# Where late attention stands on TensorE between feed-forward products, and how far ahead h products may run

## The chip, the core and the metric

The kernel runs on one core of a Trainium2 chip. A core has five engines that each go through their own instructions in order and wait for each other by semaphores: TensorE (PE) multiplies matrices into PSUM banks, VectorE (DVE), ScalarE (ACT) and GpSimd (POOL) work on tiles, and SyncE (SP) issues the transfers here. The metric is the device time of the whole program in microseconds (us); lower is better.

## What is computed

Attention with a learned decay over 4 x 8 heads of 576 x 64, and two feed-forward products behind it on 2304 tokens:

```python
def _attn_ref(q, k, v, f):
    scores = scale * np.matmul(q, k.transpose(0, 1, 3, 2))
    cum = np.cumsum(np.log(np.clip(f, 0.0001, 1.0)), axis=-1)
    decay = cum[:, :, :, None] - cum[:, :, None, :]
    scores = np.where(causal, -1000000000.0, scores + decay)
    scores = scores - np.max(scores, axis=-1, keepdims=True)
    attn = np.exp(scores)
    attn = attn / (np.sum(attn, axis=-1, keepdims=True) + 1e-09)
    return np.matmul(attn, v)

x = attn_out.transpose(0, 2, 1, 3).reshape(B * S, H * D)
h = np.maximum(x @ w_in, 0.0);  x = h * h @ w_out          
h = x @ w_in2;  g = h - np.tanh(h);  out = g @ w_out2
```

## The kernel before

**Stages.** The first feed-forward runs in eight blocks of 288 tokens (numbers 0 to 7; two blocks to a batch of eight heads), the second in five blocks of up to 512 tokens behind them. A block has 16 steps, one for each 128 of the 2048 inner columns. A step has twelve h products (L139, into the tile hp) and, two steps later, twelve y products (L165, into four tiles yp). Twelve, since every float32 factor is split into a rounded high part and a rest: high x high, low x high, high x low, over four blocks of the contraction. ACT makes relu and square of hp into gh and tmp (L149 to L151), and gl = tmp - gh (L101, the helper for every rest) is made on POOL in blocks 0 and 1 and on DVE from block 2 on. Four of a step's twelve y products read gl. hp has a single bank of PSUM in blocks 0 to 5 and three after that; gh and gl have three buffers.

**Attention beside it.** Block 2 needs the heads of batch 1, block 4 those of batch 2, block 6 those of batch 3; so attention of the later heads runs beside the feed-forward of the earlier batches. It is written as a Python generator that yields after each *piece*. A late head k (17 to 31) takes five pieces: scores of query tile 4; scores of tile 3 and the turn of tile 4; split_p(0) of head k-1, scores of tile 2, turn 3; split_p(1) of head k-1, scores of tiles 1 and 0, turn 2; turns 1 and 0, put(k), pv(k-1). After the fifth get(k) is issued. The score products are L443 and L444 into s_ps.

**From head to head.** The softmaxed P of a late head is turned in 32 x 32 blocks on DVE into T (L473, L476, L470), put stores T to DRAM (p_d, 1 MB, L479), get loads it back turned in four transfers into PTl (L485), split_p rounds it on POOL into PTh (L90) and takes the rest on DVE into PTl (L101), and pv multiplies both with V on PE into o_ps (L516 to L521). PTl, PTh and T each have one buffer, so a head's load waits for the P x V of the one before. s_ps, o_ps and o0_ps share three banks. ACT and DVE take the result out (xt L88, xs L531), and after every second head the pair's x is split and stored (x_d, L409 and L410); block 2's first load of x (xhl, L706) is issued on SP among the gets.

**What sets the order.** advance() calls as many pieces as a pace (cuts, ENDS) asks for, twice in each step of blocks 0 to 5: once behind the h products, once behind the y products. A1 is the number of the first late piece (116), total 196. The program is built twice. What is emitted before block 2 (MARK) keeps the order of the first building; behind that a planner with a timeline orders each engine's instructions, within data dependences and within the bounds that tc.issue_after sets: an instruction inside it stands behind the given one on the engine's queue. PEI[n] holds the last PE instruction emitted by the end of piece n, and SLK[j] is the slack of block j: its h products stand behind PEI[pieces so far - 1 - SLK[j]]; None sets no bound. Before the change nothing else bounds where the attention's own PE instructions stand:

```python
 660          while cnt[0] < min(to, total):
 661              next(ga, None)
 662              PEI[cnt[0]] = next(x for x in reversed(nc.cur_bb.bb.instructions) if x.engine == EngineType.PE)
 663              cnt[0] += 1
```

## Time and profile before

| | |
|---|---|
| median of 3 runs | 1089.9 us (1088.54 to 1091.76) |
| the profiled execution's own time | 1093.25 us |
| its span in the trace | 1091.5 us |
| PE busy | 1032.9 us, 95% of the span |
| DVE, ACT, POOL busy | 641.9, 526.2, 250.8 us |
| PTl loads in the chain that ended last | 6% of the span |

The span is the profiled execution from the first to the last instruction, 1.75 us shorter than its time. The trace says what each engine did when, and what the time in which it did nothing was waiting for. In the windows PEclk is the clock granted to PE as a share of 2.4 GHz; a mean between 0.5 and 1 is a mixture of the two levels, 1.2 and 2.4 GHz. Waits are named by the engine and line that waited, and by what it waited for; the chain of waits goes back from the end of the program to what released each step.

### The profile page before, as it was taken

How to read it: one execution, taken by the hardware profiler on the slowest of the kernel's cores; microseconds unless marked ns; L12 is line 12 of the kernel's file. 1: busy time of each engine (PE TensorE's matmuls, PEld its weight loads, DVE VectorE, ACT ScalarE, POOL GpSimd, SP SyncE). 2: the span in 40 equal slices, each digit the busy share in tenths (PEclk: the TensorE clock that was granted, in tenths of full speed). 3: DMA queues.
4: the chain of work that ended last, by engine and by line, in shares of the span. 5: the costliest groups of instructions: out<-in, count | busy, mean ns of one | idle time of the engine just before them, and what ended most of it. 6: DMA issues, size and time to landing. Idle time of an engine off the chain costs nothing.

```text
span 1091.5 us, 16915 instructions
## 1 busy us (share of the span) xinstructions
PE 1032.9 (95%) x6048; PEld 900.9 (83%) x6048; DVE 641.9 (59%) x1663; ACT 526.2 (48%) x1221; POOL 250.8 (23%) x357
## 2 busy tenths in 40 slices
PE   3989999999998899999989999999999999999998
PEld 3576678888998788888989999888888888888898
DVE  7799987777877677877624747763222222222232
ACT  5787777765564545646425657432222222222222
POOL 4244455555545343433310000000000000000000
PEclk9899999999999899999989999999999999999999
DMA  6556643223955657846448069100300300110010
GB/s 203 219 149 183 175 149 135 88 80 132 319 176 168 197 146 244 247 136 208 160 119 303 1 233 331 64 0 1 116 1 1 116 1 1 39 39 1 1 39 21
DMA packets 63301, 134.83 MB, mean 124 GB/s; under 512 B 6416, under 2 KB 31568, under 8 KB 61168
## 3 DMA queue, kind: packets, MB, share of 16 engines
q1 hardware_dynamic: 63216, 133.74, 38.8%
q8 instruction: 48, 0.79, 0.3%
q14 instruction: 37, 0.30, 0.1%
HBM read 93.94 MB, written 39.78 MB: 123 GB/s over the span
## 4 chain that ended last, share of the span: by engine, by line
PE 57%; DMA 9%; DVE 4%; POOL 1%; SPq 1%; ACT 1%; issue 1%; POOLq 0%; ACTq 0%; DVEq 0%
PE yp L165 27%; PE hp L139 27%; DMA PTl<-p_d 6%; DMA p_d<-T 3%; DVE PTl L101 2%; PE o_ps L519 2%; SPq L485 1%; POOL PTh L90 1%; DVE gl L101 1%; DVE T L473 1%; DVE QA L101 0%; PE s_ps L443 0%; PE s_ps L444 0%; ACT P L426 0%; PE o_ps L516 0%
## 5 line engine op out<-in xcount | busy, mean ns | idle before, releaser
L139 PE MATMUL hp<-xhl,w 128*128 128x288 f32 (+2 forms) x2496 | 453.3, 329 | 2.4 <-ACT tmp L149 1.2
L139 PEld LDWEIGHTS hp<-xhl,w 128*128 128x128 f32 x2496 | 387.6, 191 | 39.1 <-ACT tmp L149 1.7
L165 PE MATMUL yp<-ghl,w 128*128 128x512 f32 (+1 forms) x960 | 216.2, 374 | 0.0
L165 PE MATMUL yp<-gh,w 128*128 128x288 f32 x1024 | 200.6, 301 | 0.0
L165 PEld LDWEIGHTS yp<-ghl,w 128*128 128x128 f32 x960 | 168.4, 188 | 34.5
L154 DVE TENSOR_TENSOR tmp<-hp,tmp 128x512 f32<-128x512 f32 (+1 forms) x80 | 51.0, 638 | 206.6 <-ACT tmp L153 206.6
L165 PEld LDWEIGHTS yp<-gh,w 128*128 128x128 f32 x1024 | 162.4, 192 | 2.1 <-issue 1.0
L153 ACT ACTIVATE tmp<-hp 128x512 f32<-128x512 f32 (+1 forms) x80 | 44.4, 555 | 225.4 <-PE hp L139 225.4
L165 PE MATMUL yp<-gl,w 128*128 128x288 f32 x512 | 133.9, 300 | 2.6 <-DVE gl L101 1.7
L149 ACT ACTIVATE tmp<-hp 128x288 f32<-128x288 f32 x128 | 51.9, 407 | 116.2 <-PE hp L139 103.1
L426 ACT ACTIVATE P<-P,ST 128x320 f32<-128x320 f32 (+4 forms) x151 | 84.6, 562 | 34.1 <-DVE ST L417 32.9
L165 PEld LDWEIGHTS yp<-gl,w 128*128 128x128 f32 x512 | 90.6, 190 | 5.1 <-DVE gl L101 2.7
L430 POOL TENSOR_SCALAR P<-P,ST 128x448 f32<-128x448 f32 (+4 forms) x88 | 59.8, 681 | 102.8 <-DVE ST L429 61.4
L101 DVE TENSOR_TENSOR ghl<-tmp,ghl 128x512 fp32r<-128x512 f32 (+1 forms) x80 | 51.1, 638 | 47.4 <-ACT ghl L88 47.1
L101 DVE TENSOR_TENSOR gl<-tmp,gh 128x288 fp32r<-128x288 f32 x96 | 47.6, 497 | 48.0 <-ACT tmp L151 47.6
L417 DVE CUSTOM_DVE_ANT_0 P<-s_ps,mk 128x320 f32<-128x320 f32 (+3 forms) x151 | 63.6, 432 | 19.1 <-PE s_ps L444 12.2
L101 DVE TENSOR_TENSOR PTl<-PTl,PTh 128x512 fp32r<-128x512 f32 (+1 forms) x64 | 51.9, 841 | 35.1 <-POOL PTh L90 35.1
L88 ACT ACTIVATE ghl<-tmp 128x512 fp32r<-128x512 f32 (+1 forms) x80 | 47.2, 590 | 49.6 <-DVE tmp L154 49.6
L90 POOL TENSOR_SCALAR PTh<-PTl 128x512 fp32r<-128x512 f32 (+1 forms) x64 | 46.5, 752 | 56.4 <-DMA PTl<-p_d 55.7
L150 ACT ACTIVATE gh<-tmp 128x288 fp32r<-128x288 f32 x128 | 56.6, 443 | 4.0 <-PE yp L165 1.0
L151 ACT ACTIVATE tmp<-tmp 128x288 f32<-128x288 f32 x128 | 56.2, 440 | 2.4
L88 ACT ACTIVATE w<-wst 128x512 fp32r<-128x512 f32 x64 | 40.0, 625 | 29.5 <-DVE wst L123 29.4
(121 smaller groups left out, 1261.5 us busy)
## 6 DMA issues: line engine op xcount, KB each, us to landing
raw<-in_w_dram SPq DMA_DIRECT2D x64, 512.0 KB
p_d<-T SPq DMA_DIRECT2D x16, 1024.0 KB
PTl<-p_d SPq DMA_DIRECT2D x64, 256.0 KB
R<-in_qk_dram SPq DMA_DIRECT2D x24, 576.0 KB
xhl<-y_d SPq DMA_DIRECT2D x16, 512.0 KB
xhl<-x_d SPq DMA_DIRECT2D x14, 576.0 KB
y_d<-yst SPq DMA_DIRECT2D x14, 576.0 KB
VR<-in_v_dram SPq DMA_DIRECT2D x32, 160.0 KB
```

Of the source, the lines that this page charges most:

```text
L88: eng.activation(out, in_, AF.Copy)
L90: eng.tensor_scalar(out, in_, 1.0, 1.0, ALU.mult, ALU.mult)
L101: eng.tensor_tensor(out, in_, hi.bitcast(F32), ALU.subtract)
L139: nc.tensor.matmul(ps, w[:, k * 128:(k + 1) * 128], xk, start=(jj == 0), stop=(jj == 11))
L149: nc.scalar.activation(tmp, ps, AF.Relu)
L150: nc.scalar.activation(gh, tmp, AF.Square)
L151: nc.scalar.activation(tmp, tmp, AF.Square)
L154: nc.vector.tensor_tensor(tmp, ps, tmp, ALU.subtract)
L165: nc.tensor.matmul(yp[m][:, :n], w[:, c], x, start=(i == 0 and j == 0), stop=(i == NF - 1 and j == 2))
L417: nc.vector.tensor_tensor_reduce(p[:rows, a:b], ps[:rows, :b - a], mk[:rows, o:o + b - a], -0.125, 3.0e38 if mn is None else mn, ALU.add, ...
L426: nc.scalar.activation(p[:rows, :n], p[:rows, :n], AF.Exp, bias=mn, scale=-1.0, accum_out=st[:rows, 1, t:t + 1])
L430: by(n_by).tensor_scalar(p[:rows, :n], p[:rows, :n], st[:rows, 3, t:t + 1], 1.0, ALU.mult, ALU.mult)
```

## The change

Two things. SLK becomes 3 for blocks 3, 4 and 5; blocks 3 and 4 had 8, block 5 had no bound. And the late pieces are called inside tc.issue_after of the last PE instruction that stood in the program when advance() was called, which is a product of the feed-forward step just emitted; so their PE instructions stand behind it. last_pe() is the expression that was written out before.

```diff
-SLK = (None, 8, 3, 8, 8, None)
+SLK = (None, 8, 3, 3, 3, 3)
...
+    def last_pe():
+        return next(x for x in reversed(nc.cur_bb.bb.instructions) if x.engine == EngineType.PE)
+
     def advance(to):
+        ff = last_pe()
         while cnt[0] < min(to, total):
-            next(ga, None)
-            PEI[cnt[0]] = next(x for x in reversed(nc.cur_bb.bb.instructions) if x.engine == EngineType.PE)
+            with tc.issue_after(ff) if cnt[0] >= A1 else ExitStack():
+                next(ga, None)
+            PEI[cnt[0]] = last_pe()
             cnt[0] += 1
```

Both kernels have the same instructions; only their order on the engines differs, on PE from the end of block 1 on. In the rows below a name's number tells buffers and steps apart; the shape at the end is that of the moving operand, and xN is a count of like rows.

PE at the start of block 2, before the change. yp_2338 is the last y product of block 1, hp_3377 the first h of block 2, o_ps_3504 the P x V of head 16, s_ps scores of head 17:

```order
L165 MATMUL yp_2338<-gl_3360,w15_1_1949 128x288
L519 MATMUL o_ps_3504<-PTh_1610,VH_3416 128x512
L521 MATMUL o0_ps_3514<-PTl_1611,VR_3088 64x64
L443 MATMUL s_ps_3547<-QA_3409 128x320
L444 MATMUL s_ps_3547<-QB_3243 128x320
L519 MATMUL o_ps_3504<-PTh_1610,VH_3416 128x512
L519 MATMUL o_ps_3504<-PTl_1611,VH_3416 128x512
L139 MATMUL hp_3377<-xhl_3297,w0_0_480 128x288 x8
```

And with the change:

```order
L165 MATMUL yp_2338<-gl_3360,w15_1_1949 128x288
L139 MATMUL hp_3377<-xhl_3297,w0_0_480 128x288 x8
L139 MATMUL hp_3377<-xhl_3298,w0_0_480 128x288 x4
L139 MATMUL hp_3432<-xhl_3297,w1_0_610 128x288 x8
L139 MATMUL hp_3432<-xhl_3298,w1_0_610 128x288 x4
L443 MATMUL s_ps_3460<-QA_3168 128x192
L444 MATMUL s_ps_3460<-QB_3069 128x192
L443 MATMUL s_ps_3468<-QA_3168 128x64
L444 MATMUL s_ps_3468<-QB_3069 128x64
L519 MATMUL o_ps_3504<-PTh_1610,VH_3416 128x512 x2
```

Two steps of block 2's h products, and scores, now stand ahead of head 16's P x V.

PE at the end of block 3, before. gl_5163 belongs to its step 13, o_ps_5308 is the P x V of head 24:

```order
L165 MATMUL yp_4519<-gh_5162,w13_1_1758 128x288 x2
L519 MATMUL o_ps_5308<-PTh_1610,VH_5132 128x512 x2
L521 MATMUL o0_ps_5318<-PTl_1611,VR_4841 64x64
L443 MATMUL s_ps_5375<-QA_5125 128x320
L165 MATMUL yp_4516<-gl_5163,w13_1_1758 128x288
L165 MATMUL yp_4517<-gl_5163,w13_1_1758 128x288
```

And with the change:

```order
L165 MATMUL yp_4516<-gl_5163,w13_1_1758 128x288
L165 MATMUL yp_4517<-gl_5163,w13_1_1758 128x288
L165 MATMUL yp_4518<-gl_5163,w13_1_1758 128x288
L165 MATMUL yp_4519<-gl_5163,w13_1_1758 128x288
L165 MATMUL yp_4516<-gh_5223,w14_1_1855 128x288 x2
...
L165 MATMUL yp_4519<-gl_5224,w14_1_1855 128x288
L519 MATMUL o_ps_5308<-PTh_1610,VH_5132 128x512 x2
```

The y products of steps 13 and 14 now stand ahead of the P x V of head 24, which before stood ahead of step 13's four gl products.

DVE at the same place, before. The four PTl rows are head 24's rests, which need the load of its P and POOL's rounding:

```order
L101 TENSOR_TENSOR PTl_1611<-PTl_1611,PTh_1610 128x4x128
L101 TENSOR_TENSOR gl_5163<-tmp_5161,gh_5162 128x288
L101 TENSOR_TENSOR PTl_1611<-PTl_1611,PTh_1610 128x4x128
L101 TENSOR_TENSOR PTl_1611<-PTl_1611,PTh_1610 128x4x96
L101 TENSOR_TENSOR PTl_1611<-PTl_1611,PTh_1610 128x4x64
L101 TENSOR_TENSOR gl_5224<-tmp_5222,gh_5223 128x288
```

And with the change (T is that of head 25):

```order
L101 TENSOR_TENSOR PTl_1611<-PTl_1611,PTh_1610 128x4x128
L101 TENSOR_TENSOR QA_5465<-R_5168,QA_5465 64x576
L473 STREAM_TRANSPOSE T_1612<-P2_1605 128x3x4x32
L428 TENSOR_SCALAR ST_4922<-ST_4922 128x1
L101 TENSOR_TENSOR PTl_1611<-PTl_1611,PTh_1610 128x4x128
L101 TENSOR_TENSOR PTl_1611<-PTl_1611,PTh_1610 128x4x96
L428 TENSOR_SCALAR ST_4922<-ST_4922 64x1
L101 TENSOR_TENSOR PTl_1611<-PTl_1611,PTh_1610 128x4x64
L101 TENSOR_TENSOR gl_5163<-tmp_5161,gh_5162 128x288
```

gl_5163 has moved from behind the first rest to behind all four.

## Rows read from the trace of the kernel before

**Rows 1.** The page, part 1: busy us of each engine, share, instructions.

```profile
PE 1032.9 (95%) x6048; PEld 900.9 (83%) x6048; DVE 641.9 (59%) x1663; ACT 526.2 (48%) x1221; POOL 250.8 (23%) x357
```

**Rows 2.** Windows of 20 us: stretch, length, busy of PE PEld DVE ACT POOL, PEclk, DMA share, GB/s.

```profile
360.00:380.00 20.00, 15.74 (x92) 14.47 (x91) 13.09 (x37) 7.90 (x22) 9.45 (x11) 0.83 0.66 208
400.00:420.00 20.00, 18.50 (x118) 17.16 (x117) 15.03 (x55) 11.63 (x29) 10.12 (x13) 0.91 0.45 148
440.00:460.00 20.00, 18.02 (x117) 16.97 (x116) 15.89 (x50) 11.00 (x31) 9.12 (x11) 0.91 0.83 271
540.00:560.00 20.00, 16.20 (x90) 14.53 (x89) 7.35 (x15) 4.80 (x11) 4.20 (x6) 0.83 0.37 106
600.00:620.00 20.00, 20.00 (x152) 20.00 (x152) 15.05 (x29) 13.63 (x31) 0.00 (x0) 1.00 0.01 1
```

**Rows 3.** Windows of 5 us, PE alone: stretch, length, busy, PEclk, DMA share, GB/s.

```profile
345.00:350.00 5.00, 4.45 (x27) 1.00 0.00 0
365.00:370.00 5.00, 3.86 (x13) 0.51 0.49 167
```

**Rows 4.** Waits, 262 to 575 us: who waits for whom, us in all, times, longest.

```profile
POOL PTh L90 <- DMA PTl<-p_d: 55.7, 14, 11.7
...
PE o_ps L519 <- POOL PTh L90: 16.6, 9, 4.3
...
PE yp L165 <- DVE gl L101: 1.7, 2, 1.0
```

**Rows 5.** Chain of waits, 320 to 575 us, heads 19 to 21: start, us, what.

```profile
328.85 2.33 POOL PTh L90 x3
...
344.46 0.63 POOL PTh L90
...
352.82 5.11 DMA p_d<-T
...
359.32 5.97 DMA PTl<-p_d
365.47 0.63 POOL PTh L90
```

**Rows 6.** The same chain, head 29.

```profile
517.59 0.63 POOL PTh L90
518.26 0.49 PE o_ps L519
```

**Rows 7.** Timeline of SP's DMA queue, the load of head 29: start, us, what.

```profile
510.04 1.74 SPq L485 DMA_DIRECT2D PTl<-p_d  x4
```

**Rows 8.** Groups by line, 325 to 560 us: busy, mean ns, then idle before.

```profile
L101 DVE TENSOR_TENSOR PTl<-PTl,PTh 128x512 fp32r<-128x512 f32 (+2 forms) x52 | 43.0, 856 | 33.8 <-POOL PTh L90 33.7
...
L101 DVE TENSOR_TENSOR gl<-tmp,gh 128x288 fp32r<-128x288 f32 x48 | 24.8, 517 | 10.8 <-ACT tmp L151 10.6
...
L101 DVE TENSOR_TENSOR QA<-R,QA 64x576 fp32r<-64x576 f32 x10 | 11.6, 1161 | 0.3
```

**Rows 9.** Chain of waits, 540 to 640 us: the last P·V, and block 7.

```profile
561.51 0.43 PE o_ps L519
...
630.59 1.60 PE hp L139 x12
```

**Rows 10.** Timeline of SP's queue: a get, and the loads of x for blocks 2 and 6.

```profile
268.92 1.79 SPq L485 DMA_DIRECT2D PTl<-p_d  x4
...
271.23 0.98 SPq L706 DMA_DIRECT2D xhl<-x_d  x2
...
566.16 1.95 SPq L706 DMA_DIRECT2D xhl<-x_d  x2
```

**Rows 11.** Timeline of PE at the start of block 2: head 16's P·V, block 2's h.

```profile
278.79 0.46 PE L519 MATMUL o_ps<-PTh,VH 128*128 128x512 f32 x1
...
281.12 1.23 PE L139 MATMUL hp<-xhl,w 128*128 128x288 f32 x8
```

## The prediction

> **What bounds the kernel now.** I first read the page's busy shares and its slices. TensorE (PE) is busy 95% of the span, DVE 59%, ACT 48%, POOL 23% [rows 1], so the end is set by PE, and the question is what keeps PE from its products. The slices say where. In blocks 2 to 5, from about 279 to 562 us, late attention and feed-forward share PE; behind 562 us PE is dense (20.00 busy of 20 at 600 us) [rows 2]. In the shared part two things cost time: waits, and stretches in which the granted clock lay below full. 360 to 380 us was busy for 15.74 of 20 us at a mean clock of 0.83 of 2.4 GHz, that is with a part of it at the lower level, 1.2 GHz; the slices at 400 and 440 have 0.91, that at 540 has 0.83 [rows 2]. Those four lose 3.4 + 1.8 + 1.8 + 3.4 = 10.4 us (20 us times what is missing to 1.00). A fall follows a pause: 365 to 370 us, behind the longest wait, has 0.51 [rows 3].
>
> The view of waits names the pauses. Between 262 and 575 us the P·V products (o_ps, L519) wait 16.6 us in nine places for POOL's rounding of P (PTh, L90), the longest 4.3 us, and that rounding itself waits for the load of the turned P back from DRAM (PTl<-p_d, 55.7 us). The second feed-forward products wait 1.7 us for gl on DVE [rows 4]. So the thing that ends last in this part is a loop from head to head: P turned on DVE, stored (put), loaded (get), rounded on POOL, its rest taken on DVE, multiplied on PE.
>
> The chain of waits shows two lengths of that loop. The **long** one runs where the turns and the put of a head stand on DVE behind the rests of the head before. From one rounding to the next it took 15.6 us in one head (328.85 to 344.46) and 21.0 us in the next (to 365.47), of which the put came 8.4 us behind the rounding, its store took 5.1, the load 6.0 [rows 5]. The **short** one runs where the put is long done and only the load waits for the buffer: load issued at 510.04, rounding at 517.59, products at 518.26, some 8 us [rows 6, 7], and with the product ahead of it (2.5 us, eight of 0.49 and less [rows 6]) about 11 from head to head.
>
> PE's own work in this part I count from the order at dense durations: twelve products of 128x288 take 1.60 us [rows 9], a step of h and y 3.2; five blocks of 16 steps from the start of block 2 to that of block 7 make 256 us, the late heads at some 4 us each 58.6, together 314.6. The trace needed 351.8 (278.8, where the P·V of head 16 starts, to 630.6 us [rows 9, 11]). So **37.2 us are lost**, and the order leaves PE's own work as it was. The whole question is what is lost with the new order.
>
> **The change part by part.** Nothing is removed or added; the same instructions stand otherwise on each engine. Before, P·V products and scores slid ahead between feed-forward products as the planner found room; now they stand whole behind the last feed-forward product emitted, and in blocks 3 to 5 h products may no more run ahead than three pieces. Effect one: feed-forward is spread evenly. Own work between the starts of successive P·V was 10.5 to 21 us, uneven; in the new order heads 17 to 31 have 17.8, 17.4, 10.0, 19.0, 13.7, 16.9, 16.9, 18.5, 19.9, 21.6, 20.0, 17.3, 13.6, 17.2, 11.4 (head 22, for one: 2.5 of P·V, 1.6 of scores, four steps of 3.2). That is 11 us more cover in sum, and as much less dense work behind the last head. What each wait becomes is loop minus cover.
>
> *Long loops.* Heads 17, 18, 20, 22, 23 and 30 have the long loop and less cover than it. I take loops of 19.0 to 21.6 us, nearer to the 21.0 than to the 15.6 [rows 5], since in the new order the turns that the put waits for stand behind the rests, with gl among them, in all of these heads: 1.15 + 1.6 + 2.6 + 3.85 + 3.6 + 2.8 = 15.6 us. With 15.6 everywhere nothing is left (0), with 21.0 the sum is 3.2 + 3.6 + 2.0 + 4.1 + 4.1 + 3.8 = 20.8. Heads 24 to 28 have cover for it.
>
> *Short loops.* Heads 19, 21, 29 and 31 have 10.0 to 13.6 us of cover against some 11 to 14: 2.45 + 0.55 + 1.8 + 1.0 = 5.8 us (21's load stands behind two stores of yst on SP's queue). Bounds: 1 us (all at 11) and 8 (all at head 29's present pace, two us more each for 19 and 31).
>
> *The feed-forward's gl on DVE.* This is new. gl and the rests of PTl are both DVE's: 517 ns and 856 ns, four rests to a head, and one QA of 1161 ns among them [rows 8]. DVE goes in order, so a gl queued behind the rests waits until POOL has rounded, that is until the load has landed. Before, the gl of block 3's step 13 stood behind the first of head 24's rests, and PE had that head's P·V ahead of its gl products anyway. Now it stands behind all four, while on PE its four products stand *ahead* of that P·V. PE gets there 16.1 us behind the start of P·V of head 23 (18.5 less 2.4 of gl and gh products); the loop, taken at 17, brings the rounding, then the rests (4 x 0.86), QA and gl end 5.9 us later: 22.9 - 16.1 = 6.8 us. In the same way block 4's steps 1 and 2 wait 3.3, step 8 0.5, step 13 2.6: 13.2 us in all. Bounds: with a loop of 15.6 the first is 5.4, with 21.0 10.8, and the others run from 0 to 7: 5.4 to 18. Queued behind the waiting gl product are all of PE's later products, the P·V of that head too, so nothing hides it.
>
> *The two loads of x.* The h products of block 2's first steps now stand ahead of head 16's P·V, and need xhl, whose load was issued at 271.23, behind a get at 268.92 [rows 10]. Before, they ran at 281.12, with P·V from 278.79 on ahead of them [rows 11]. If the load landed just then, PE waits 2.3 us, if it was there long before, nothing; with up to 0.6 for the one bank of hp the bounds are 0 and 2.9. I take 2.5, since the first h products came in the middle of a P·V, as if something had just landed. At the other end, block 6's x depends on the last P·V, which ended at 561.9; the load was issued 4.2 us later [rows 9, 10], and if it takes as long as the load of a P (6.0 [rows 5]) it lands 10.2 us behind that end. The feed-forward left to cover it is 7.5 us by the order: up to 2.7, none at best, 1.5 taken.
>
> Sum of waits: 15.6 + 5.8 + 13.2 + 2.5 + 1.5 = **38.6 us**, against 37.2 lost before, clock included.
>
> *Clock.* A pause can drop the clock, and the products behind it then take longer. In front of a head whose loop is late, PE only waits less; around heads 24 to 28 PE has cover and is the bound, and there the slow products lengthen the end. A slice such as 360 to 380 lost 3.4 us [rows 2]; I take one of that kind, 3 us, with 0 and 10.4 (as much as before in all) as ends.
>
> 38.6 + 3 - 37.2 = **+4 us** (4.4). Against the profiled execution's own 1093.25 us that is 1097; that execution lay 3.3 us above the median of 1089.9, so the median becomes 1094.
>
> **The Trainium skill on the clock.** What the rows show: 365 to 370 us ran at 0.51 behind the 4.3 us wait, while 345 to 350 us, behind the pause that ended with the rounding of 344.46 [rows 5], kept 1.00 at 4.45 busy us of 5 [rows 3]. The Trainium skill, "TensorE: Matmul & The Clock Gate", section "What's actually happening", says that the throttled clock is the default and activity releases it, with only two levels. By that, every long pause that the new order makes would be paid twice, and it speaks against an order that gathers feed-forward and attention into solid stretches with pauses between. This trace bears it out in part: one of the two pauses was paid twice. If all did so, the time would be that of the third rival.
>
> **The rivals.**
> *Faster.* The long loop is as short as the 15.6 us [rows 5] in all heads. Then the six long waits vanish (15.6), and the gl waits, which hang on the same loop, about halve (6). 1089.9 + 4 - 21.6 = 1072; halfway 1081. It decides by how soon the put follows the rounding: under some 5 us (8.4 in [rows 5]) it is faster. For it: even spreading is what a fixed loop wants, the unevenness before put 10.5 and 21 us of cover beside each other. Against it: DVE's queue gets fuller between rounding and turns, and gl's wait does not need the long loop.
> *No difference.* The loops are the bound in both programs; their sum over 15 heads is the same, and the waits only change place. 1090, up to 3 us either way.
> *Slower by the clock.* Three or four falls like those in the slices at 360 and 540 us, 3.4 each [rows 2] and not hidden in heads 22 to 28, in place of one: 1094 + 7 to 10 = 1101 to 1104. For it: the 6.8 us wait for gl is longer than any of today's. Against: before, falls were hidden behind the next loop as well.
> *It doesn't do what it says.* The order shows at blocks 2 and 3 that it does; 1090.
>
> **How the numbers follow.** Forecast (1091 to 1098) 0.33, no difference 0.22, slower by the clock 0.18, faster 0.25, not done 0.02. A measurement tells 0.3%, 3.3 us, from no change: under 1086.6 is faster, over 1093.2 slower. All but none of the faster case lies under 1086.6, and some of the no-difference one's edge: 0.26. Slower: 0.18 and four fifths of the forecast, 0.44. Same: 0.30. The range runs from 1080, which leaves out half of the faster case, to 1102, which leaves out some of the clock's: 1080 to 1102; for slower or equal alone it is 1088 to 1102.
>
> **What would show it right or wrong.** In the changed profile: gl products at the end of block 3 and in block 4 waiting for DVE gl, some 13 us in all against 1.7 (the step of which I am surest); P·V waiting for POOL some 21 us, in more places than nine and with shorter ones; dense PE from about 11 us nearer to the end on; a first wait at block 2's start for the load of x. If waits for POOL fall below 10 us, the loops are shorter than taken and the faster rival holds. If the sum of waits is as I say and the time is over 1100, it is the clock, and slices behind 6 us waits will have 0.5 to 0.8. If gl's waits aren't there, the order of DVE doesn't bind as I read it, and the forecast is too high by their sum.

## The result: 18 us slower, where 4 were forecast

The changed kernel takes 1107.75 us (median of 4, 1107.17 to 1108.90) against 1089.5 us before: ratio 1.0149, interval 1.0128 to 1.0171. The sign was forecast, the size was not, and the time lies above the range (1080 to 1102). Measured again beside another run the ratio was 1.0168.

The profiled execution took 1108.23 us, its span is 1106.3 us. The busy times of the engines are those of before to within 0.5% [rows 1], so the same work is done with more holes in it:

```profile
PE 1035.4 (94%) x6048; PEld 902.6 (82%) x6048; DVE 643.8 (58%) x1663; ACT 527.3 (48%) x1221; POOL 251.9 (23%) x357
```

The windows of the changed kernel (columns as in [rows 2]) show where. In 320 to 340 us pauses and a low clock (0.82) come together, 420 to 440 us holds the longest pause (PE busy for 13.57 us), and behind 600 us PE is dense as before:

```profile
320.00:340.00 20.00, 15.29 (x78) 12.91 (x77) 10.35 (x31) 7.53 (x20) 5.89 (x10) 0.82 0.51 152
420.00:440.00 20.00, 13.57 (x99) 12.94 (x97) 13.55 (x40) 8.82 (x24) 8.68 (x11) 0.96 0.69 207
440.00:460.00 20.00, 18.22 (x109) 17.03 (x110) 8.13 (x22) 7.93 (x20) 4.01 (x7) 0.87 0.67 203
500.00:520.00 20.00, 16.99 (x108) 15.81 (x108) 13.13 (x37) 9.06 (x23) 7.39 (x10) 0.91 0.40 112
600.00:620.00 20.00, 20.00 (x152) 20.00 (x152) 14.18 (x29) 15.76 (x36) 0.00 (x0) 1.00 0.99 374
```

The waits of the changed kernel, 262 to 600 us (columns as in [rows 4]), against that group:

```profile
POOL PTh L90 <- DMA PTl<-p_d: 67.5, 15, 12.1
...
PE o_ps L519 <- POOL PTh L90: 12.1, 9, 2.4
...
PE yp L165 <- DVE gl L101: 11.0, 5, 6.4
...
PE hp L139 <- DMA xhl<-x_d: 3.4, 2, 2.1
PE yp L165 <- DVE ST L428: 3.0, 1, 3.0
```

P·V waits less for POOL than before (12.1 for 16.6 us, in nine places both times), where the forecast had some 21 us in more places than nine; gl products wait 14.0 us where they waited 1.7 (the last line is a gl product's wait too, put down to a small instruction just behind that gl on DVE); and h products wait for x.

To count what is lost altogether I took the start of every PE product between the last product of block 1 and the first h of block 7, and by how much each interval exceeds the dense interval of the same two forms. An excess of over 0.3 us is a wait; smaller ones are slow products (at the lower clock above all), and the smallest are put together as a rest:

| | waits | of them P·V, gl and other y, h | slow products | rest | sum |
|---|---|---|---|---|---|
| before | 24.8 | 20.7, 3.1, 1.0 | 12.0 | 1.8 | 38.6 |
| changed | 36.9 | 16.3, 14.9, 5.7 | 17.6 | 2.1 | 56.6 |

The loss is 18.0 us larger (the dense intervals themselves sum to 0.9 less); block 1 ended 2.7 us earlier, so the first h of block 7 stands 14.4 us later (644.80 for 630.43). That is nearly all of the difference of the two profiled executions (15.0 us; the one profiled before lay 3.75 us above its median of 1089.5). A second profile of the changed kernel (changed_again, below), counted in like manner, has 39 us of waits, of them P·V 18, gl and other y 13, h 8: differences of 2 to 3 us between single profiles are no more than their spread.

The same difference can be read from the chain of heads. The first rounding of a head's P on POOL is its mark. Before, for heads 16, 24 and 31:

```profile
278.07 1.21 POOL L90 TENSOR_SCALAR PTh<-PTl 128x512 fp32r<-128x512 f32 x2
...
425.84 1.20 POOL L90 TENSOR_SCALAR PTh<-PTl 128x512 fp32r<-128x512 f32 x2 [3.40 <-DMA PTl<-p_d]
...
552.43 0.62 POOL L90 TENSOR_SCALAR PTh<-PTl 128x512 fp32r<-128x512 f32 x1 [7.65 <-DMA PTl<-p_d]
```

Changed, for heads 16, 17, 24, 28 and 31:

```profile
274.26 2.91 POOL L90 TENSOR_SCALAR PTh<-PTl 128x512 fp32r<-128x512 f32 x4 [0.76 <-DMA PTl<-p_d]
...
300.44 2.91 POOL L90 TENSOR_SCALAR PTh<-PTl 128x512 fp32r<-128x512 f32 x4 [7.56 <-PE yp L165]
...
433.32 2.11 POOL L90 TENSOR_SCALAR PTh<-PTl 128x512 fp32r<-128x512 f32 x3 [5.48 <-DMA PTl<-p_d]
...
531.05 4.20 POOL L90 TENSOR_SCALAR PTh<-PTl 128x512 fp32r<-128x512 f32 x4 [0.38 <-DMA PTl<-p_d]
...
580.03 2.11 POOL L90 TENSOR_SCALAR PTh<-PTl 128x512 fp32r<-128x512 f32 x3 [5.59 <-DMA PTl<-p_d]
```

From head 16 to 31 it takes 274.4 us before and 305.8 changed: 31.4 us more in fifteen loops. From the last rounding to block 7 it takes 78.0 and 64.8: 13.2 us less, since more feed-forward is done by then. The chain of heads pays 31 us and gets 13 back; it also starts 3.8 us earlier.

### The profile page after: what moved, and what is told of

The parts are those of the page before. It is cut to its first block, busy times and chain, and to the rows that moved or that the text cites. A ratio compares the mean times of both kernels' runs of the same rounds, so it can differ in the third digit from the quotient of the medians.

```text
span 1106.3 us, 16909 instructions
## 1 busy us (share of the span) xinstructions
PE 1035.4 (94%) x6048; PEld 902.6 (82%) x6048; DVE 643.8 (58%) x1663; ACT 527.3 (48%) x1221; POOL 251.9 (23%) x357
## 4 chain that ended last, share of the span: by engine, by line
PE 65%; DMA 14%; DVE 12%; issue 2%; POOL 2%; SPq 2%; ACT 1%; POOLq 0%; ACTq 0%; DVEq 0%
PE yp L165 28%; PE hp L139 28%; DMA PTl<-p_d 7%; DMA p_d<-T 3%; DVE PTl L101 3%; PE o_ps L519 3%; SPq L485 1%; DMA R<-in_qk_dram 1%; DMA xhl<-x_d 1%; DVE P L417 1%; POOL PTh L90 1%; PE o_ps L345 1%; PE s_ps L443 1%; DVE QA L101 1%; DVE gl L101 1%
## 5 line engine op out<-in xcount | busy, mean ns | idle before, releaser
L165 PEld LDWEIGHTS yp<-gl,w 128*128 128x128 f32 x512 | 90.7, 191 | 17.2 <-DVE gl L101 12.5
L149 ACT ACTIVATE tmp<-hp 128x288 f32<-128x288 f32 x128 | 51.9, 405 | 106.3 <-PE hp L139 97.7
L417 DVE CUSTOM_DVE_ANT_0 P<-s_ps,mk 128x320 f32<-128x320 f32 (+3 forms) x151 | 63.6, 430 | 27.5 <-PE s_ps L444 21.8
L101 DVE TENSOR_TENSOR gl<-tmp,gh 128x288 fp32r<-128x288 f32 x96 | 51.4, 535 | 29.3 <-ACT tmp L151 28.9
```

The lines of the kernel that those rows point to most:

```text
L101: eng.tensor_tensor(out, in_, hi.bitcast(F32), ALU.subtract)
L149: nc.scalar.activation(tmp, ps, AF.Relu)
L165: nc.tensor.matmul(yp[m][:, :n], w[:, c], x, start=(i == 0 and j == 0), stop=(i == NF - 1 and j == 2))
L417: nc.vector.tensor_tensor_reduce(p[:rows, a:b], ps[:rows, :b - a], mk[:rows, o:o + b - a], -0.125, 3.0e38 if mn is None else mn, ALU.add, ...
```

## The experiments

**What needed no run.** With SLK alone changed, every engine has the order of the kernel before, row for row; with the queueing of the late pieces alone, every engine has that of the changed kernel. So SLK's new numbers move nothing, and all that was measured is due to the queueing.

In the runs that keep an order, the kernel is built once more with each engine's instructions chained in the order of the changed kernel (or the one before); the edit is then the only thing that moves. In the diffs `row` is that order, `at` names instructions in it (h, y, gl by step counted from block 0; rest, pv by head), and `place` gives each one's place on its engine. Where a queueing bound of the change would forbid the edit, it is left out of that last building. In free_five, free_ten, early_only, late_only and before_more_lead no order is kept: there the planner orders everything behind block 1 anew, so more may move than the edit. All ratios are against the kernel before, measured in the same rounds.

### Does the gl wait itself cost?

At the end of block 3 the changed kernel shows the wait that the order had shown. DVE, then PE:

```profile
433.97 1.09 DVE L101 TENSOR_TENSOR PTl<-PTl,PTh 128x512 fp32r<-128x512 f32 x1 [4.97 <-POOL PTh L90]
...
436.60 2.54 DVE L101 TENSOR_TENSOR PTl<-PTl,PTh 128x512 fp32r<-128x512 f32 x2
...
439.12 0.40 DVE L101 TENSOR_TENSOR PTl<-PTl,PTh 128x256 fp32r<-128x256 f32 x1
439.46 0.44 DVE L101 TENSOR_TENSOR gl<-tmp,gh 128x288 fp32r<-128x288 f32 x1
```

```profile
439.95 1.33 PE L165 MATMUL yp<-gl,w 128*128 128x288 f32 x4 [6.43 <-DVE gl L101]
...
443.96 1.06 PE L519 MATMUL o_ps<-PTh,VH 128*128 128x512 f32 x2
```

The gl product waited 6.43 us (forecast 6.8), for four rests that had waited for the load.

```diff
+    def edit(row, at):
...
+        for u in range(16, 32):
+            pos = place(row, at)
+            pv = min(pos[x] for x in at["pv", u])
+            rs = sorted(at["rest", u], key=pos.get)
+            gs = [at["gl", s][0] for s in range(32, 96) if min(pos[x] for x in at["y"][12 * s:12 * s + 12][2::3]) < pv and pos[at["gl", s][0]] > pos[rs[0]]]
+            if gs:
+                g = max(gs, key=pos.get)
+                xs = [x for x in rs if pos[x] < pos[g]]
+                row = [x for x in row if x not in xs]
+                k = row.index(g) + 1
+                row = row[:k] + xs + row[k:]
...
```

> The changed kernel with its whole order kept on every engine, except that on DVE the four rests of P of heads 24, 25, 26 and 27 stand directly behind the gl of the steps (61 and 62; 65 to 67; 72; 77, counted from block 0) whose products stand ahead of those heads' P.V on PE. In the trace of the changed kernel gl products wait 14.9 us in the loop part (against 3.1 before). Theory A: these waits lie on the path, since PE is the bound there, and with the slow products behind them they are worth 11 to 17 us: 1091 to 1097 us, gl waits under 4 us. Rival B: the loop from head to head is late anyway and the wait only moves to P.V of heads 24 to 28: 1103 us or more, with P.V waits grown by about as much as the gl waits shrink.

Measured 1104.92 us, ratio 1.0115 (1.0074 to 1.0155), 1.0149 for the changed kernel: some 4 us less, not 11 to 17, and the intervals overlap. Of the 14.9 us of gl and other y waits 8.6 were left; P·V's stood at 18.6 us for 16.3 and h's at some 8.6 for 5.7, as in the second profile of the changed kernel. Theory A was wrong, mostly, and the time is Rival B's. The trace of this run says why a wait was left, at step 77. POOL, then DVE, then PE:

```profile
504.67 2.05 POOL L91 TENSOR_SCALAR PTh<-PTl 128x512 fp32r<-128x512 f32 x4 [10.86 <-DMA PTl<-p_d]
506.69 0.64 POOL L442 TENSOR_SCALAR P<-P,ST 128x448 f32<-128x448 f32 x1
```

```profile
507.37 0.71 DVE L485 STREAM_TRANSPOSE T<-P 128x512 f32<-128x512 f32 x1 [5.31 <-POOL P L442]
508.00 1.63 DVE L102 TENSOR_TENSOR gl<-tmp,gh 128x288 fp32r<-128x288 f32 x1
```

```profile
509.69 1.33 PE L174 MATMUL yp<-gl,w 128*128 128x288 f32 x4 [3.47 <-DVE gl L102]
```

POOL's rounding waited 10.86 us for the load; the normalising of another head's P stood behind it on POOL, that head's turn waited for this on DVE, and gl stood behind the turn. So the load's lateness was carried on by three queues in turn, each of which held work behind it that doesn't need that load.

### Does the start of block 2 cost?

PE of the changed kernel at the start of block 2, and SP's put of head 17:

```profile
276.05 1.32 PE L139 MATMUL hp<-xhl,w 128*128 128x288 f32 x8
278.68 0.80 PE L139 MATMUL hp<-xhl,w 128*128 128x288 f32 x4 [1.30 <-DMA xhl<-x_d]
280.03 1.86 PE L139 MATMUL hp<-xhl,w 128*128 128x288 f32 x12 [0.56 <-ACT tmp L149]
...
281.99 0.28 PE L444 MATMUL s_ps<-QB 68*128 68x64 f32 x1
282.10 0.70 PE L519 MATMUL o_ps<-PTh,VH 128*128 128x512 f32 x2
```

```profile
288.82 0.33 SPq L479 DMA_DIRECT2D p_d<-T  x1
```

Head 17's last scores stand behind two steps of h that wait for x, and its put is issued at 288.82; before it was issued at 278.03, ahead of head 16's P·V:

```profile
278.03 0.33 SPq L479 DMA_DIRECT2D p_d<-T  x1
```

First the h products alone were put behind head 16's P·V, in the kept order.

```diff
+        row = behind(row, at["h", 32] + at["h", 33], at["pv", 16])
+        e = max(row.index(x) for x in at["exp", 17, 0])
+        row = behind(row, [x for x in at["act", 32] + at["act", 33] if row.index(x) < e], at["exp", 17, 0])
+        m = max(row.index(x) for x in at["min", 17, 0])
+        row = behind(row, [x for x in at["gl", 32] + at["gl", 33] if row.index(x) < m], at["min", 17, 0])
```

> The changed kernel with its whole order kept, except that the h products of block 2's first two steps stand on PE behind the P.V of head 16 (in the changed kernel they stand ahead of it and of head 17's last scores and wait for x), with their squares on ACT and gl on DVE behind those scores' exp and row minimum. Theory A: what the place of these h products costs is more than their own wait of 2.2 us, since head 17's last scores and with them its put are held too (put at 288.8 against 278.0 before) and every later head starts from there: 5 to 10 us less than the changed kernel, 1098 to 1103. Rival B: the loop has slack by then and only the 2.2 us come back: 1105 to 1107.

Measured 1111.14 us, ratio 1.0169 (1.0133 to 1.0205): no gain, and neither theory. In its trace head 17's put came later still (at 292.45 us, 16.1 us behind the rounding of head 16, where it was 14.6). Its last scores did end sooner, 1.0 us behind that rounding instead of 8.0. But its last turns stand on DVE behind the gl of block 2's first two steps, and the h products of these now came behind a P·V that waited for its own rests: the first gl waited 4.68 us for ACT and started at 288.18. The edit put one hold in the place of another, and shows that the scores alone do not set the put.

> Both edits in one. If gl behind the rests and the held start of block 2 are two separate costs on the path, the gains add: 1083 to 1091 us, at or under the kernel before. If the start of the heads decides both (an earlier head 24 makes the gl wait short by itself), it is no better than the better of the two alone: 1091 or more.

Both edits in one: 1105.02 us, ratio 1.0115 (1.0076 to 1.0153), as gl_first alone; since x_later did not bring the put forward, this says nothing on adding up.

Undoing the queueing for the first five late pieces (head 17's scores, head 16's P·V) does bring it forward:

```diff
-            with tc.issue_after(ff) if cnt[0] >= A1 else ExitStack():
+            with tc.issue_after(ff) if cnt[0] >= A1 + 5 else ExitStack():
```

> The change without its effect on the first five late pieces: head 17's scores and head 16's P.V may slide ahead again, as before the change; every later piece is bound. In the changed kernel head 17's last scores stand behind block 2's first h products, which wait for x, and its put comes 13.5 us later (counted from the last product of block 1) than before; every head behind follows. Theory A (the lost lead): the heads start some 10 us earlier and most of that stays to the end, since the loop decides from head to head: 1093 to 1100 us, 0.2 to 0.9% over the kernel before. Rival B: the later loops take it up (each waits for scores held behind its own feed-forward products): 1103 or more.

Measured 1104.12 us, ratio 1.0095 (1.0057 to 1.0133). Head 17's put is issued at 275.91 us, its loop (rounding of 16 to rounding of 17) is 16.8 us instead of 26.2, and the chain from 16 to 31 is 299.5 us, 6.3 less. That is less than Theory A gave, and by the ratios 0.5 to 0.7% of the time (the intervals just overlap with the first measurement of the changed kernel, and lie apart from the second): these pieces are a part of the answer. That head 17's lead is carried to the end is not shown. From head 16 to 24 the chain is no shorter (159.7 us for 159.1), since later loops are longer again, most that of head 24 (23.1 us for 17.2, its put 8.5 us behind the rounding ahead of it instead of 4.5); the 6.3 us lie between heads 24 and 25 (16.7 for 23.3). With ten pieces free (`A1 + 10`):

> The same with the first ten late pieces free (heads 17 and 18, P.V of 16 and 17). Before the change head 18's put stood right behind the rounding of head 17 (0.2 us), in the changed kernel 7.8 us behind it. Theory A: with that lead too another 3 to 6 us come back against the run with five: 1089 to 1096. Rival B: as the run with five, within 2 us.

1106.06 us, ratio 1.0085 (1.0053 to 1.0117): no difference from five, as Rival B said.

### Which half of the heads?

```diff
-            with tc.issue_after(ff) if cnt[0] >= A1 else ExitStack():
+            with tc.issue_after(ff) if A1 <= cnt[0] < A1 + 40 else ExitStack():
```

> The change for heads 16 to 23 alone: late pieces up to P.V of head 23 stand behind the last feed-forward product, later ones are free again as before the change. Theory A: the gl waits of heads 24 to 27 (steps 61, 65, 72, 77; 13 us with what they slow) do not arise, those of the start and heads 17 to 22 stay: 1094 to 1101 us. Rival B: the held start alone is what costs (P.V of head 24 starts 20 us later in the changed kernel than before, and everything behind it follows): 1104 or more.

```diff
+            with tc.issue_after(ff) if cnt[0] >= A1 + 40 else ExitStack():
```

> The change for heads 24 to 31 alone: the pieces behind P.V of head 23 are bound, the ones before are free as before the change; seven gl products stand on PE ahead of the P.V whose rests stand ahead of their gl on DVE, as in the changed kernel. Theory A (the early half alone costs): within 5 us of the kernel before. Rival B (the gl waits of heads 24 to 27 cost by themselves, some 14 us of waits and 4 of slow products): 1101 or more.

Bound for the early heads alone (P·V of 16 to 23, scores of 17 to 24): 1107.82 us, ratio 1.0137 (1.0100 to 1.0174), its Rival B. Bound for the late ones alone (P·V of 24 to 31): 1099.23 us, ratio 1.0058 (1.0034 to 1.0082), between its two theories. The early half costs nearly all by itself, although it has none of the four gl waits; the late half, which has them all, costs 6 us. The waits of early_only, 262 to 600 us:

```profile
PE o_ps L519 <- POOL PTh L90: 17.8, 12, 3.7
PE yp L165 <- DVE gl L101: 1.8, 2, 1.4
```

Counted as above, the waits of early_only up to head 24's rounding (some 22 us) are those of the changed kernel (24 and 20 in its two profiles, 13 before), and those behind it (some 11 us) are those of the kernel before (11; changed 14 and 19). So each half costs where it is bound. Whether the two costs add can't be told: 1.95% in sum, give or take 0.4, against 1.5 to 1.7%.

### Is it the loop?

Half of P's store and load is left out of the computation, in either kernel, with the order kept:

```diff
-        by("put").dma_start(p_d[u % 2], PT["t"].rearrange("p b a s j -> p (b a s j)"))
+        n = 64 if ROW and u > UT else 128
+        by("put").dma_start(p_d[u % 2][:n], PT["t"].rearrange("p b a s j -> p (b a s j)")[:n])
...
-            by("get").dma_start(dst.bitcast(F32), src[:, :, b])
+            n = 2 if ROW and u > UT else 4
+            by("get").dma_start(dst.bitcast(F32)[:, :n], src[:, :n, b])
```

> The changed kernel with its whole order kept on every engine; put and get of heads 17 to 31 move half of P only (64 of 128 rows out, half of PTl in), so that part of P is left out of the computation and the store (5.1 us) and load (6.0) of each loop are about half as long. Theory A: what the changed order loses hangs on the loop from head to head (P.V waiting for POOL, gl behind the rests and turns on DVE, which wait for the load). With some 5 us less in each loop most of the 36.9 us of waits go, and the slow products behind them: 1070 to 1082 us. Rival B: the order costs by itself (products held behind products, h behind x, DVE's queue full) and the loop has little to do with it: 1095 or more.

> The kernel before with its whole order kept and the same half store and load for heads 17 to 31 (part of P is left out). Theory A: 24.8 us of waits and 12 us of slow products hang on the loop here as well; most go: 1062 to 1072 us, and the two kernels with half transfers lie 4 to 12 us apart in place of 18. Rival B (the changed order costs by itself): the distance stays at 15 us or more.

Measured in the same rounds: 1072.71 us (ratio 0.9819, 0.9796 to 0.9842) with the changed order, 1069.44 us (0.9783, 0.9758 to 0.9807) with the order before. With loops that are shorter the two orders lie 3.3 us apart where they lay 18 (their intervals overlap), and all else is equal. Both times lie in the ranges of their Theory A. This is the run that decides: the changed order costs by way of the loop from head to head, and by nothing else of that size. The longer chain is not the cost in itself: from head 16 to 31 it still takes 17.6 us more in the changed order here (268.6 for 251.0), of which 11.3 come back at the end. It costs where PE has to wait for it. The waits that are left, changed order, then order before:

```profile
PE hp L145 <- DMA xhl<-x_d: 3.7, 3, 1.5
PE yp L174 <- DVE gl L102: 3.6, 3, 1.6
```

```profile
PE yp L174 <- DVE gl L102: 4.0, 2, 2.1
...
PE o_ps L535 <- POOL PTh L91: 0.4, 1, 0.4
```

P·V hardly waits for POOL any more, and slow products fall to 7.8 and 5.4 us.

### Is it the clock?

Behind the pause at head 18 the changed kernel's products ran at the lower clock (PEclk 0.75 and 0.57 in 320 to 325 and 325 to 330 us). Products without use were put into five pauses.

```diff
+        for n in range(FILL.get(u, 0)):
...
+            nc.tensor.matmul(ps, wf[:, :128], wf, start=True, stop=True)
```

> The changed kernel with its whole order kept and extra products without use put on PE where it waited longest: nine of 512 columns (about 2 us) into the bank of o_ps ahead of P.V of heads 18, 19 and 22, forty and twenty of 288 columns (5.3 and 2.7 us) into the next hp ahead of the gl products of steps 61 and 77. They only use time in which PE stood still. Theory A: the clock falls because PE pauses; with the pauses filled the slow products behind these five (some 10 us of excess in the trace) go, of which 4 to 8 us show at the end: 1100 to 1104. Rival B: the low clock has another cause, or lies in time that the loops hide: 1106 to 1110, with the same slices at 0.82 to 0.93.

Measured 1118.21 us, ratio 1.0237 (1.0201 to 1.0272): slower, for a reason of the experiment's own. The fill at step 61 needed hp's only bank, and waited longer than the pause that it was to fill:

```profile
443.70 7.32 PE L144 MATMUL hp<-w 128*128 128x288 f32 x40 [7.34 <-ACT tmp L160]
```

So the fills at heads 18, 19 and 22 were run alone, which use the bank of the P·V behind them.

> The changed kernel with its whole order kept and nine products without use of 512 columns (2.05 us) on PE ahead of P.V of heads 18, 19 and 22 alone, where PE stood for 2.6, 2.4 and 2.4 us and products ran at the lower clock behind it (some 6 us of excess by the end of head 22's P.V). The fills at steps 61 and 77 of the run before, which waited for their own bank, are left out. Theory A: the low clock comes from the pause and goes with it, but between heads 17 and 23 the loop decides, and only what shortens a P.V that the next load waits for shows: 1 to 3 us less than the changed kernel. Rival B: all of it shows, 5 us or more less. Rival C: nothing, or the 6 us that the fills take are lost: as the changed kernel or above.

Measured 1106.16 us, ratio 1.0113 (1.0082 to 1.0144). The windows of this run:

```profile
320.00:340.00 20.00, 19.98 (x136) 18.57 (x136) 14.43 (x48) 11.33 (x31) 6.69 (x9) 1.00 0.79 225
380.00:400.00 20.00, 18.41 (x121) 16.42 (x120) 15.06 (x45) 10.45 (x26) 7.70 (x10) 1.00 0.58 174
```

0.82 has become 1.00 there (0.94 has in 380 to 400), so the low clock did come from the pauses. Against the two measurements of the changed kernel that is 4 and 6 us less, between Theories A and B, with intervals that overlap; heads 16 to 24 took 156.5 us instead of 159.1 and 160.1. Together with the half transfers this makes the low clock mostly a follower of the loop's pauses between heads 17 and 23. What it costs behind the gl waits of steps 61 and 77 (0.50 in 440 to 445 us, 0.66 in 512 to 517), where PE is the bound, was not measured, since the fills there failed.

### What lengthens the loops of heads 24 to 28?

From the rounding of head 24 to that of 28 it takes 76.5 us before and 97.7 changed. In the changed kernel P·V of heads 24 to 27 starts 10.6, 11.0, 6.7 and 8.0 us behind the rounding of its P, and the one buffer of PTl is held until it ends, 15.4, 13.5, 9.2 and 11.4 us behind the rounding (7.2 to 9.0 before).

```diff
+        for u in range(24, 32):
+            pos = place(row, at)
+            pv = min(pos[x] for x in at["pv", u])
+            r = min(pos[x] for x in at["rest", u])
+            ys = [x for s in range(32, 96) if pos[at["gl", s][0]] > r for x in at["y"][12 * s:12 * s + 12] if pos[x] < pv and x in at["y"][12 * s:12 * s + 12][2::3]]
+            ys = [x for x in ys if pv - pos[x] <= 20]
+            if ys:
...
+                row = ahead(row, sorted(at["pv", u], key=row.index), min(ys, key=pos.get))
```

> The changed kernel with its whole order kept, except that on PE the P.V of heads 24 to 27 stands ahead of the gl products (steps 61, 67, 72, 77) that wait on DVE behind those heads' rests; the rest of PE, and every other engine, as in the changed kernel. There P.V started 10.6, 11.0, 6.7 and 8.0 us behind the rounding of its P (0.7 to 3.3 before the change), and since PTl has one buffer the loads of the heads behind started later by that: roundings of heads 24 to 28 lie 97.7 us apart in sum (76.5 before). Theory A: the held P.V is what lengthens these loops; they come to 85 us or less, and the time to 1097 to 1104. Rival B: the gl waits as such; they stay short of P.V's rests only by a little (gl_first had ratio 1.0115): as gl_first, 1104 to 1106. Rival C: no gain, since the loop then waits in the next head: 1106 or more.

Measured 1108.27 us, ratio 1.0147 (1.0121 to 1.0173): Rival C. The y waits fell to 4.1 us and P·V's rose to 25.0; the four loops still took 95.6 us. Its waits for P·V, 262 to 600 us:

```profile
PE o_ps L533 <- POOL PTh L91: 11.0, 9, 2.6
PE o_ps L533 <- DVE PTl L102: 4.6, 5, 2.4
...
PE o_ps L533 <- POOL P L442: 2.3, 1, 2.3
```

The gl wait as such is not what lengthens these loops by 21 us (gl_first, with the rests behind gl, brought them to 90.9). On the held buffer this run says little, since the edit moved the starts of P·V more than the ends: its later products still waited for the rests, and PTl came free 13.5, 13.5, 8.6 and 10.1 us behind the rounding. The chain of the changed kernel says more. In it the loads of heads 26 and 27 follow directly on the stores of their P, that of head 25 on the P·V of head 24:

```profile
449.77 6.63 DMA PTl<-p_d
...
469.99 6.62 DMA p_d<-T
477.94 6.14 DMA PTl<-p_d
...
494.00 5.54 DMA p_d<-T
500.87 6.05 DMA PTl<-p_d
```

The loads of heads 26, 27 and 28 were issued 6.6, 6.0 and 4.4 us after the buffer had come free, that of head 25 just as it did. So head 25's loop hangs on the held P·V and the other three on their puts. For these the trace points to the scores: before, the last scores of heads 17 to 31 ended 0.4 to 7.2 us ahead of the rounding of the head before; in the changed kernel those of heads 17, 26, 27 and 28 end 8.0, 7.1, 1.9 and 1.0 us *behind* it, and their puts come 14.6, 13.4, 9.7 and 10.4 us behind that rounding. Four of the five longest loops are theirs (26.2, 27.7, 22.8, 23.9 us; the fifth, head 25's 23.3, waits with its load for the held P·V of head 24, and pv_first brought it to 20.7). For head 17 free_five shows that the queueing holds the put, and x_later that the scores are not alone in it; for heads 26 to 28 it is argued and was not tried.

The same edit in the kernel with the first five late pieces free:

> The kernel with the first five late pieces free (ratio 1.0095), and in it the P.V of heads 24 to 27 ahead of the gl products that wait behind their rests. Theory A: lost lead and held P.V are the two ways by which the changed order lengthens the chain of heads; with both undone the ratio comes to 1.000 to 1.006. Rival: 1.008 or more, and something else in the bound order (scores that stand behind feed-forward products in heads 18 to 23) holds most of it.

1103.17 us, ratio 1.0099 (1.0073 to 1.0124): as free_five alone, so its rival held. Last, the two edits that had seemed to gain, beside the changed kernel in the same rounds:

> The changed kernel itself, on the same chip and in the same rounds as the run beside it, since the partial gains so far (ratios 1.0095 with the first five pieces free, 1.0115 with the gl ahead of the rests) were measured apart from it (1.0149). All theories: 1.012 to 1.018.

> The kernel with the first five late pieces free, its whole order kept, except that on DVE the rests of heads 24 to 27 stand behind the gl of steps 62; 65 to 67; 72; 77 that PE reads ahead of those heads' P.V. Theory A (lost lead and gl behind rests are two costs, both real): ratio 1.004 to 1.008, clear of the changed kernel beside it. Rival B (the gl wait only moves to the next loop): as with the first five free alone, 1.009 to 1.011. Rival C (the gains of both were noise between sessions): within 0.3% of the changed kernel beside it.

1110.88 us (ratio 1.0168, 1.0142 to 1.0194) and 1100.10 us (1.0079, 1.0052 to 1.0106). The intervals are apart: 10.8 us, half of what the change costs, come back with head 17's pieces free and gl ahead of the rests. Most comes with the free pieces (free_five 1.0095); what gl adds cannot be told from nothing. Heads 16 to 24 still take 158.3 us.

### More lead for the kernel before

```diff
-CUT = (25, 44, 61, 2)
+CUT = (25, 44, 61, 6)
```

> The kernel before with the pace moved by four pieces: six late pieces in place of two by the end of block 1. If lead of the heads over the feed-forward is what counts in both kernels, the chain of heads starts some 5 to 10 us earlier and ends so, with more feed-forward left to cover the end: 1080 to 1087 us, 0.3 to 0.9% under the kernel before. Rival: block 1 has no room (its own steps then wait for scores and banks), or the pace of block 2 gives the lead back: 1088 or more.

1103.11 us, ratio 1.0073 (1.0050 to 1.0096): the rival. Head 17's rounding came 13.0 us behind head 16's instead of 16.2, but head 18's 25.9 instead of 17.6, and from 16 to 24 it took 158.6 us instead of 147.8. An earlier pace of emission moves the wait to the next head. No kernel here that computes the whole beats the one before.

### The chain of heads

The table has the us between first roundings of heads, and from head 31's to block 7, each from one profiled execution (that of late_only lay 7 us above its median, that of early_only 5 us below):

| | ratio | 16 to 24 | 24 to 31 | 31 to block 7 |
|---|---|---|---|---|
| before | 1 | 147.8 | 126.6 | 78.0 |
| changed | 1.0149 | 159.1 | 146.7 | 64.8 |
| changed_again | 1.0168 | 160.1 | 145.5 | 63.9 |
| early_only | 1.0137 | 159.6 | 128.7 | 76.7 |
| late_only | 1.0058 | 149.5 | 147.7 | 65.1 |
| free_five | 1.0095 | 159.7 | 139.8 | 63.8 |
| free_ten | 1.0085 | 157.2 | 142.2 | 63.6 |
| free_five_gl_first | 1.0079 | 158.3 | 137.4 | 63.3 |
| gl_first | 1.0115 | 159.6 | 139.6 | 63.8 |
| pv_first | 1.0147 | 159.2 | 144.2 | 64.8 |
| before_more_lead | 1.0073 | 158.6 | 130.6 | 76.9 |
| half_after | 0.9819 | 138.9 | 129.7 | 64.6 |
| half_before | 0.9783 | 136.0 | 115.0 | 75.9 |

Binding the early heads costs 11 to 12 us in the first column, of which the end gives back 1. Binding the late ones costs 20 in the second, of which 13 come back in the third.

Long and short loops go, in both kernels, with how far a head's put comes behind the rounding of the head ahead of it. In the kernel before, six of the fifteen puts came over 7 us behind it (heads 21, 22, 24, 26, 28 and 30), and their loops took 21.8 us on average, the other nine 16.0. In the changed kernel it is nine puts (heads 17, 18, 20, 22, 23 and 25 to 28) with 23.4 us, the other six 15.9. So the 31 us are three more long loops and somewhat longer ones. Of the puts of heads 17 to 24 three are so late before and in late_only, and five in every other kernel of the table but half_before, before_more_lead among them. This is read from the traces; no run moved the puts alone.

## Why the forecast was right in sign and wrong in size

- *Nothing changes but order.* Right, and SLK's part of the change moves nothing at all, which the forecast took for a part of the effect.
- *P·V waits* (long loops 15.6, short 5.8 us, together 21.4): measured 16.3 us, less than before (20.7) where more was forecast. The missing part is in the slow products, see *Clock*.
- *gl waits* (13.2 us, the first of them 6.8): measured 14.9 with other y waits, the first 6.43. Right in kind and in sum. But they are worth far less than their length: in pv_first, where they are taken away, P·V waits instead and the time stays.
- *The loads of x* (2.5 and 1.5 us): some 2.2 and 2.3. Right as waits. The forecast missed that head 17's last scores, and gl ahead of its turns, stand behind the same h products, by which its put comes 14.6 us behind the rounding.
- *Sum of waits* 38.6 us: measured 36.9. The nearness is in part luck: P·V was taken 5.1 us too high, gl and h 3.4 too low together.
- *Clock*: **this term failed.** It was taken as 3 us; slow products measured 17.6. The 37.2 us on the other side of the difference held all the slow products of the kernel before (12.0 by the count above), so the forecast in effect let them fall from 12.0 to 3. Like with like, the slow products and the rest came to 19.7 us in the changed kernel, against 13.8 before. 36.9 + 19.7 - 38.6 - 2.7 (the earlier end of block 1, not forecast) is 15.3, about what the profiled executions show. With the 10.4 that stood as the upper end, the sum would have been +12.
- *The ground for the 3 us* was that slow products ahead of a late head only shorten its wait. That holds where the loop was well taken. The forecast reckoned a wait as loop less dense cover; counted so, from one start of P·V to the next with waits and slow products together, eight of the ten long and short loops (heads 17, 20 to 23 and 29 to 31) lost some 18.5 us in sum where 17.35 were taken. At heads 24 to 28, where the 3 us were meant since PE is the bound there, slow products came to some 6 us beside 14 of waits (13.2 taken).
- *The loops of heads 18 and 19* were taken too short, 19.0 and 12.45 us; they took 21.8 and 15.6, and lost some 4.5 and 5.8 us where 1.6 and 2.45 were taken. Head 18's put came 7.8 us behind the rounding, and behind its wait PE ran at the lower clock into head 19's loop. The short loop was reckoned at about 11 us from one load and 2.5 us of P·V; from rounding to rounding the head that it was read from (29) took 15.3 us before. P·V lasted 3.9 to 8.0 us in heads 16 to 23, since its later products wait for the rests on DVE, and the next load waits for its end. The loop of head 17 was missed by most, 26.2 us for 19.0, at little cost to PE: the P·V of head 16 was held back by 7.8 us with it, behind products that had to be done anyway.
- *The faster rival* wanted puts within 5 us of the rounding. They did in four of fifteen heads (19, 21, 24 and 31); in the others they came 5.4 to 14.6 us behind it. It fell.
- *No difference, the waits only change place*: wrong as a forecast, but right in that a wait taken away comes back elsewhere, as pv_first shows.
- *Slower by the clock* (1101 to 1104): the low clock was there, in windows of 0.82 and 0.87, and the sign that the prediction named for it (0.5 to 0.8 behind a 6 us wait) came true with 0.50 in 440 to 445 us. But waits grew by 12.1 us and slow products by 5.6, and the half transfers show that both hang on the loop; the number came nearer than the mechanism.

Open is what makes five of the eight puts up to head 24 late in every kernel with queueing there that computes the whole, so that heads 16 to 24 take 156 to 162 us where 147.8 were enough. free_ten, with the heads 17 and 18 free, still has 157.2; and since before_more_lead has 158.6 without any queueing, it need not be the queueing as such.

## What to carry to other kernels

Where two streams share an engine and one has a long round trip through other queues, look first at the length of that round trip and at how far the stream runs ahead of it. Here the pauses on the shared engine were its shadow, and taking one away mostly made another. Work that slides forward between the other stream's instructions can start the next round trip earlier, so queueing it behind "the last product emitted" can take more than order away (here the first five pieces were worth some 0.5 to 0.7%). And in a difference of two sums the same kinds of loss must stand on both sides.

## What the runs showed of the hardware

A pause alone did not tell whether the clock fell (1.00 is 2.4 GHz, 0.50 is 1.2 GHz, and a window between has both). In the changed kernel the 6.43 us wait at 439.95 was followed by 0.50 in 440 to 445 us, that of 2.4 us at head 18 by 0.57 in 325 to 330; behind the wait of 1.2 us at head 20 (360.54) the window 360 to 380 us kept 1.00. Between these it went either way: a wait of 2.26 us at head 22 (395.98) was followed by 0.76 in 395 to 400 us, and in the kernel before one of 2.13 us at head 20 (345.13) by 1.00 in 345 to 350 [rows 3]. Filling the pauses ahead of heads 18, 19 and 22 with products without use kept the clock at 1.00 there; but a fill that has to wait for a bank made the pause longer (7.34 us). The Trainium skill, "TensorE: Matmul & The Clock Gate", section "What's actually happening", has the low clock as the state that activity releases; these traces agree in that products in the pauses kept the clock up which fell without them.
